# Attention with three full heads, then a maxout layer, on one core: keys and queries of four halves transposed by DMA, a head's long score tile on both row halves of the array, and a new order of all instructions

## The chip, the core and the metric

The kernel runs on 1 core of one Trainium2 chip. The metric is the device time of one execution, in microseconds (us). Before the change it is 176.41 us, the median of 3 runs (176.35 to 176.73).

## The reference

Four batches of 768 tokens have 8 heads of 64 columns. A head is either full (causal attention) or a stream head, which sees the first 4 keys and the last 64. Which heads are full is an input; here there are three of them. The tokens' head outputs are joined to x (3072 x 512), which goes through a maxout layer:

```python
scores = scale * np.matmul(q, k.transpose(0, 1, 3, 2))
mask = np.where(retr[0, :, 0, 0, None, None], full_mask, stream_mask)
a = np.exp(scores - max)                      # masked scores are -1e9
a = a / (np.sum(a, axis=-1, keepdims=True) + 1e-09)
attn = np.matmul(a, v)
...
x = attn.transpose(0, 2, 1, 3).reshape(B * S, H * D)
out = np.maximum(x @ w1, x @ w2) @ w_out      # w1, w2: 512 x 1024; w_out: 1024 x 512
```

All inputs and the output are float32. The kernel works in bfloat16 with float32 sums.

## The kernel before, in words

**Halves.** The work is cut into 8 halves (b, h): batch b, tokens 0 to 383 (h = 0) or 384 to 767 (h = 1). They are taken in the order of `HALVES`: (0,0), (1,0), (0,1), (1,1), (2,0), (2,1), (3,0), (3,1). The heads of a batch go in four pairs, `SLOTS = ("FF", "FS", "SS", "SS")`: pair 0 holds two full heads, pair 1 a full and a stream head, pairs 2 and 3 stream heads. One head of a pair has rows 0 to 63 of the TensorE array, the other rows 64 to 127. n = 4 b + pair numbers the pairs.

**One half.** The loads of q, k and v (`load_half`, L413) fill one of three slots of `ld`. A half in `LONG` takes q and k in one 768 KB transfer each (L426), with runs of 768 bytes; any other half, and every v but the first, takes three 256 KB transfers (L439), with runs of 256 bytes. Casts (`cast_qk`, `cast_v`; L366 on ScalarE, L368 on VectorE and GpSimd) bring them to bfloat16. Then q and k of each pair are transposed, so that the 64 columns of a head lie on partitions. That is done in one of two ways: for the halves in `TURNED_BY_DMA`, (2,1), (3,0) and (3,1), by two DMA transposes per pair, one for q and one for k (`turn_by_dma`, L666); for the other five by TensorE (`turn`, L645, six 128x128 transposes per pair) and a copy out of PSUM (`unturn`). `attend` (L1018) lays the 128x128 score blocks out in tiles of two PSUM banks (`GROUP_A`, `GROUP0`, `GROUP1`). Per tile there are the score matmuls (`scores`, L915), two exponentials (ScalarE, L930), the masks (VectorE, L955), and the sums with v (`weighted`, L980). When a pair is done, VectorE divides by the sums (L997, L1007) and writes x.

**Row halves.** A score matmul has 64 rows. `scores` alternates between the two banks of a tile; where these belong to the two heads of a pair, the two matmuls use different row halves. In `GROUP1`, used for every h = 1, tile 5 holds only blocks of pair 1's full head, so both of its banks use rows 0 to 63.

**The layer.** x is transposed (by TensorE at L1103 for the first three halves, by one DMA transpose at L1122 for the others). The layer is computed as relu(x(w1 - w2)) w_out + x(w2 w_out): `up` (L1206) multiplies by w1 - w2, which VectorE makes at L1139 (`w` in rows), with a relu behind it (L1231, L1233); `down` (L1263) does twelve matmuls of 512 columns per 128 tokens, four on x with w2 w_out (`w2o`) and eight on the relu's output with w_out (`wob`). The product w2 w_out is made once, at the start: VectorE or ScalarE casts w2 (`w2b`), TensorE transposes it (L1156), the transposes are copied out (`w2t`), and 32 matmuls multiply by w_out (L1183).

**What sets the order.** `Order.run` takes a string, `PLAN`: each token names a step, its engine (p TensorE, a ScalarE, v VectorE, g GpSimd, s SyncE) and its PSUM banks. Each engine executes its own steps in this order, and waits only for what they need. A token xN is a dummy matmul of 128 columns (L353) on bank N, which computes nothing that is used; there are 133. SyncE issues nearly all transfers, in the order of its tokens.

Of the kernel before, what the change touches and what calls it, by code (L numbers as in the profile page):

```python
# [22 lines left out]
def f(j, *queries):  # L23
    return tuple(("f", j, i) for i in queries)


def d(i):
    return (("d", i),)
# [10 lines left out]
def one(p, hh, blocks):  # L39
# [47 lines left out]
    ([one(1, 0, f(0, 3, 4, 5) + f(3, 4)), one(1, 0, f(1, 3, 4, 5) + f(3, 5))], []),  # L87
    ([one(1, 0, f(2, 3, 4, 5)), one(1, 1, END1 + d(5))], [(1, 1, 0, 2, 2)]),
# [27 lines left out]
class Order:  # L116
# [38 lines left out]
0s x0*3 1s x0*5 2s x0*36 3s 66a 50v x0*3 28a 64v x0 48g x0 58a x0 68p0 26a 25g x1*2 52p1 56a 69v 44p2 x3 4s  # L155
60p3 53v x4*2 45v x4*5 8s 29a 67g 65v x4*4 57a x4 49g x4*4 27a x4 59v x4*2 70p4 51a x5 46p5 x6 71v x6 54p6 47a
62p7 x0*2 61v x0*2 63a x0 72p01 55v x2*4 74a x2*3 9s 31g x2 30v x2*3 76p24 33g 73a 6s 32v 81p53 85p76 34a 35g
89p10 83a 75v 37g 87a x3*3 84v x3*4 91a x3*2 36g 93p36 90a x0 13s 126v x0*2 40p0 95a 11s 92v 38p1 86a 122v 82a
5g 42p6 41a 39v 123p7 78a 43v 127p5 124a 80v x0 108p0 97p1 128v 77a 99p 139p4 100v 16s 130a 134v 137p6 152p7
101v 94a 135p5 102v 79v 131p2 136a 96v 98p1 103p 88v 138p3 132a 113p 104v 10v 107p5 109p 105v x2*4 7g x2*2  # L160
106v x2*7 110v x2*2 114v x2*2 112v x2*6 111v x2*6 14s 140p 115v 116v 143p 141p 144p 15s 125v 117p2 153p 118a
121v 154p 12g 119p1 142p 120a 145p 215p5 148p 216a 150p 149a 19s 133v 146p 151a 155p 147a 213p0 129v 226p2
214a 156v 224p1 18s 157a 181g 167a 197g 159v 227a 220p5 195v 169a 183v 225a 163p3 173p4 221a 201p6 164v 222p0
202a 174v 187p7 20s 170a 158g 209p2 168a 188v 160g 184a 182g 175p1 223a 165p5 210v 198g 189p3 176a 211p6 196g
17s 166v 190a 203p4 179v 177v 240p70 212a 193v 244p21 204v 247p53 423s 241a 219p6 191v 245a 205v 246a 207v
242a 218p4 249a 243v 229p 248a 251v 21s 250v 252p72 234p 254a 253a 24s 172v 161g 162a 255v 256p10 186a 199g
200v 185a 260p35 264p27 258a 171g 230p 194v 262a 208g 178v 261a 237p 206v 426s 266a 263v 257a 268p0 269p 238a
180v 217p5 259v 265a 239s 192a 270v 267v 273p3 274p 272v 279p7 235a 278p1 275v 427s 292g 271v 280p 309a 284p
228p 276v 293g 319a 285v 281v 308g 277v 299a 296p6 424s 282v 298g 318a 231p 286v 297a 283v 322p2 287v 551s
232a 302p4 323v 290p0 303a 288p3 312p1 289v 291a 359p67 363p52 425s 324v 360a 366p40 326v 340p3 304v 306v 365a  # L170
313v 368a 334p6 22s 437g 453a 452v 336p2 341a 314v 457g 236s 335v 444a 330p0 436a 430v 23s 367a 441v 431v
332p1 361a 445v 337v 338p3 331a 362v 333a 342p6 449a 316v 339v 364a 676s 434g 328p4 443v 451a 450g 369p72 343v
329a 372p01 377p35 428g 435v 550s 371a 380p64 373a 349p2 429v 378a 442v 375v 382a 432p0 379a 438p3 383v 673s
321g 301v 446p4 300a 294g 350p 370a 439v 381a 295g 552s 320g 374a 351p 447v 305g 433a 325g 396p5 307v 397p
327g 310a 448v 384p76 388p31 386a 392p40 440v 398p 671s 311v 393a 399p 376v 354p6 317v 315a 233s 400v 385a
402v 807s 403p4 401v 394a 404p 387v 405p 355p 389a 395v 390a 356p 406v 391v 804s 561a 562g 409p7 407v 411p
571a 408v 410p5 581g 565p0 412v 572a 556v 555g 415p 344p3 357a 554s 413v 416v 566a 414v 345p 418v 352a 417v
559p1 582a 674s 421p4 560a 575p6 346p 576v 422a 806s 419p7 347a 489p05 420v 493p21 490a 496p46 672s 454p3 495a
# [12 lines left out]
620v 748p75 706s 811g 838a 751p64 613p 746a 812v 827v 749a 828v 816s 614p 817v 750a 837v 818v 753a 778p0 752a
615v 754p17 747a 759p54 756a 762p62 841s 716p3 761a 758v 764a 720p7 842s 763a 765v 710p4 755a 721a 712p2 757v
822s 717a 779p 711a 713v 780p 760a 781p 785p6 832s 782v 714p1 783v 784v 786p 715a 787p 766p73 788v 770p42 821s
843v 768a 774p50 845v 789v 726p1 772a 790v 767a 815s 825v 823v 718p3 771a 769v 731p6 775a 831s 833v 835v 776a
773v 724p2 719a 777v 722p7 616s 725a 931s 792p4 723a 797p 791p5 798v 793p 727p 800v 928s 794v 799v 728p 795v
796v 935s 878p03 729v 882p27 885p45 880a 732p 886a 730s 887a 733p 888v 884a 889v 883a 801s 736p1 879a 734v
881v 890p34 894p57 892a 898p20 930s 906p6 895a 893v 907p 911p4 900a 908v 737p 932s 909v 896a 910v 899a 902p50
897v 738p 891a 901v 903a 904a 916p7 905v 739a 912p 917p6 913v 922p 918p 929s 851p2 914v 915v 853p3 923v 852a
919v 925v 933s 855p5 921v 854a 924v 859p0 621s 920v 856v 934s 868p1 860a 847p4 926s 950a 959v 936g 942a 857p2
937g 943a 849p3 958g 951a 858a 861p6 941s 850v 848a 863p7 862a 864p 940s 960a 953v 952g 869p 944a 939v 961a  # L200
957a 938v 965v 870p 945v 949g 865p 947s 871a 978p5 866a 946s 997p02 979v 1001p43 999a 1004p61 970p7 955s 998a
1002a 976p5 1000v 1006a 948v 954s 980p2 971v 1005a 977v 1034p0 1003a 966p4 981a 1035p 963s 967v 1007p17
1010p65 1009a 1036p 1008a 972p3 962s 956v 1012a 1037p 968p2 973v 1011a 735s 1014v 1015p47 1038v 969v 740s
1018p15 1022p36 1016a 1039v 872s 974p2 1040v 1024a 867s 964v 1013v 873p4 1020a 975v 1017a 1021v 1041p0 1023a
1026p65 1019a 1030p27 1025v 1042p 1028a 1043p 874p 1031a 1044v 1046v 1032a 1045v 1047p3 1027a 875p 1033v 1029v
1049p 992p1 876a 1050v 1052v 877s 1048p5 1051v 1053p 993p 1054v 1055v 1056v 994p 1057s 1094v 982p2 995v 983p
996s 1095p7 987p0 1096v 988p 989p 984p 990a 991s 1062p6 985a 1072p4 986s 1063a 1058p3 1073v 1068p5 1059a
1079p1 1069a 1084p0 1060p2 1064p6 1061v 1070p4 1065a 1066p3 1071a 1074p7 1067v 1075p 1080p 1081p 1076p
# [3 lines left out]
1082v 1085p 1083s 1077a 1086p 1078s 1089p5 1087v 1090p 1091p 1088s 1092a 1093a  # L212
# [15 lines left out]
NLD = 3  # L228
NQB = 6
NQK = 8  # L230
# [6 lines left out]
LONG = ((0, 0), (0, 1), (1, 0), (1, 1), (2, 0))  # L237
# [65 lines left out]
def tile_three_full_heads(  # L303
# [109 lines left out]
    def load_half(b, hf, kinds=(0, 1, 2)):  # L413
# [45 lines left out]
        if b in V_BY_DMA:  # L459
            order_ = [(t, i) for t, i in order_ if t < 2]  # L460
# [1269 lines left out]
```

## Time and profile before

| what | value |
|---|---|
| median of 3 runs | 176.41 us (176.35 to 176.73) |
| the profiled execution: span from its first to its last instruction | 175.4 us |
| what the median has beyond that span | 1.0 us |
| instructions | 4945 |
| granted TensorE clock, mean | 0.997 |
| moved by DMA | 36.14 MB, 206 GB/s in the mean |

Times in the trace count from the span's start. A row of the timeline gives a start, a length and the merged instructions; a row of the windows gives, for a stretch, the busy time of each engine with its count of instructions, then the granted clock, the DMA share and GB/s. TensorE's matmuls overlap, and "mean ns of one" is longer than the step from one to the next; the price of a matmul in a row of many is therefore taken from start to start.

### The profile page before, as it was taken

Reading aid. Unit: us, or ns where it says so; the run is one execution under the profiler, and the core shown is the slowest. Engines: PE = TensorE matmul, PEld = TensorE weight load, DVE = VectorE, ACT = ScalarE, POOL = GpSimd, SP = SyncE. Lnnn points to the kernel's source line nnn. Section 1 sums busy time; section 2 is a strip of 40 time slices with the busy share of each in tenths; the row PEclk is TensorE's granted clock in tenths of the full one; section 3 lists DMA queues with packets and bytes.
Section 4 is the critical chain, followed back from the end, with each engine's and each line's share of the span. In section 5 each row is a group of like instructions: output and inputs, shape, how many; then the busy total and the mean of one; then the engine's idle time right before and its main releaser. Section 6 shows DMA issues by size and latency. Waiting matters only on the chain.

```text
span 175.4 us, 4945 instructions
## 1 busy us (share of the span) xinstructions
PE 168.5 (96%) x1795; PEld 105.5 (60%) x1816; DVE 122.0 (70%) x331; ACT 126.3 (72%) x280; POOL 34.2 (19%) x78
## 2 busy tenths in 40 slices
PE   7999799999999999999999999999999999999993
PEld 7976575655665666666656545764565566545542
DVE  5579899686999997887858666666884168941211
ACT  3499807998999998999997669795858598405200
POOL 5732132422414613040200240000012000000000
PEclk9999999999999999999999999999999999999998
DMA  4999999999899999992597993339999334453004
GB/s 129 334 371 389 387 382 333 214 312 298 201 248 258 281 300 211 234 283 71 152 190 192 238 225 76 71 69 237 213 242 176 67 87 153 154 153 122 0 7 179
DMA packets 77661, 36.14 MB, mean 206 GB/s; under 512 B 59202, under 2 KB 72514, under 8 KB 77634
## 3 DMA queue, kind: packets, MB, share of 16 engines
q1 hardware_dynamic: 77488, 35.73, 78.4%
q8 instruction: 15, 0.25, 0.6%
q14 instruction: 12, 0.10, 0.2%
q10 hardware_dynamic: 146, 0.07, 0.1%
HBM read 25.17 MB, written 6.29 MB: 179 GB/s over the span
## 4 chain that ended last, share of the span: by engine, by line
PE 85%; DMA 6%; POOL 3%; issue 2%; DVE 2%; POOLq 0%; ACT 0%; DVEq 0%; SPq 0%; ACTq 0%
PE ps L1263 36%; PE ps L1206 24%; PE ps L915 9%; PE ps L980 8%; DMA ld<-in_moe_w_dram 6%; PE ps L645 3%; PE ps L1183 3%; POOL tab L1605 1%; PE ps L1103 1%; DVE at L955 1%; PE ps L353 1%; DVE x L1007 0%; POOL tab L1619 0%; POOL g L705 0%; POOLq L1670 0%
## 5 line engine op out<-in xcount | busy, mean ns | idle before, releaser
L930 ACT ACTIVATE at<-ps 128x512 bf16<-128x512 f32 (+2 forms) x134 | 64.1, 573 | 6.4 <-PE ps L915 6.2
L1206 PE MATMUL ps<-xt,w 128*128 128x384 bf16 x256 | 45.8, 326 | 0.0
L1263 PE MATMUL ps<-wob,g 128*128 128x512 bf16 (+2 forms) x192 | 44.7, 370 | 0.4
L955 DVE TENSOR_TENSOR at<-at,tab 128x1024 bf16<-128x1024 bf16 (+5 forms) x56 | 29.9, 549 | 10.7 <-ACT at L930 10.3
L1206 PEld LDWEIGHTS <-w 128*128 128x128 bf16 x256 | 23.9, 98 | 16.0 <-issue 0.4
L1263 PEld LDWEIGHTS <-g 128*128 128x128 bf16 x200 | 18.0, 98 | 18.8 <-issue 0.2
L1231 ACT ACTIVATE g<-ps 128x384 bf16<-128x384 f32 x37 | 18.0, 502 | 11.1 <-PE ps L1206 10.0
L1233 DVE TENSOR_SCALAR g<-ps 128x384 bf16<-128x384 f32 x27 | 14.6, 550 | 15.8 <-PE ps L1206 15.7
L1263 PE MATMUL ps<-w2o,xt 128*128 128x512 bf16 (+2 forms) x90 | 23.5, 370 | 0.5
L1007 DVE TENSOR_TENSOR x<-ps,rez 128x192 f32 x64 | 22.7, 355 | 1.6
L368 POOL CAST qb<-ld 128x384 bf16 (+1 forms) x28 | 13.2, 505 | 50.5 <-DMA ld<-in_q_dram 30.6
L366 ACT COPY ot<-ps 128x512 f32<-128x512 f32 (+1 forms) x18 | 10.4, 575 | 17.0 <-PE ps L1263 16.8
L980 PEld LDWEIGHTS <-at 128*128 128x128 bf16 x477 | 18.6, 97 | 6.3 <-DVE at L955 1.2
L980 PE MATMUL ps<-vb,at 128*128 128x65 bf16 x387 | 20.4, 193 | 0.4 <-DVE at L955 0.4
L915 PE MATMUL ps<-qk 64*128 64x128 bf16 (+1 forms) x330 | 18.4, 228 | 0.2
L915 PEld LDWEIGHTS <-qk 64*128 64x128 bf16 x330 | 12.2, 94 | 7.2 <-issue 4.7
L368 DVE COPY qk<-ps 128x384 bf16<-128x384 bf16 (+1 forms) x17 | 11.3, 693 | 3.9 <-PE ps L645 3.8
L1263 PEld LDWEIGHTS <-xt 128*128 128x128 bf16 x100 | 8.9, 97 | 8.5
L366 ACT CAST qb<-ld 128x384 bf16 (+1 forms) x31 | 11.8, 440 | 2.8 <-DMA ld<-in_q_dram 1.7
L353 PE MATMUL ps<-warmer 128*128 128x128 bf16 x133 | 12.1, 256 | 1.4 <-POOL warmer L1655 1.2
L353 PEld LDWEIGHTS <-warmer 128*128 128x128 bf16 x133 | 10.5, 118 | 1.7 <-POOL warmer L1655 1.2
L368 POOL CAST vb<-ld 128x192 bf16 x15 | 5.7, 406 | 24.6 <-DMA ld<-in_v_dram 24.5
(74 smaller groups left out, 161.4 us busy)
## 6 DMA issues: line engine op xcount, KB each, us to landing
ld<-in_v_dram SPq DMA_DIRECT2D x21, 256.0 KB, 5.0
ld<-in_moe_w_dram SPq DMA_DIRECT2D x4, 1024.0 KB, 11.8
out_dram<-ot SPq DMA_DIRECT2D x16, 256.0 KB, 3.4
ld<-in_q_dram SPq DMA_DIRECT2D x5, 768.0 KB, 7.3
ld<-in_k_dram SPq DMA_DIRECT2D x5, 768.0 KB, 8.4
ld<-in_k_dram SPq DMA_DIRECT2D x9, 256.0 KB, 4.5
ld<-in_q_dram SPq DMA_DIRECT2D x9, 256.0 KB, 4.9
ld<-in_moe_w_out_dram SPq DMA_DIRECT2D x4, 512.0 KB, 10.6
```

What stands on the lines that cost most here:

```text
L353: nc.tensor.matmul(banks[e][:, 0:128 * m].rearrange("p (m c) -> p m c", m=m), lhsT=warm, rhs=warm.unsqueeze(1).to_broadcast([128, m, 128]) ...
L366: nc.scalar.copy(out=out, in_=in_)
L368: eng[e].tensor_copy(out=out, in_=in_)
L915: nc.tensor.matmul(to.rearrange("p (i c) -> p i c", c=128), lhsT=lhsT, rhs=q_of(n, i, m)[rows], start=True, stop=True, skip_group_check=True,)
L930: nc.scalar.activation(out=at[:, bk, 0:w], in_=bank(("ps", b, hf, t), part=bk)[:, 0:w], func=ACT.Exp, scale=scale,)
L955: eng[e].tensor_tensor(out=at, in0=at, in1=tbl, op=ALU.mult)
L980: nc.tensor.matmul(po[:, hh, i - NT * hf, :], lhsT=ats[:, T["at", b, hf, t] % NAT, bk, e * 128:(e + 1) * 128], rhs=rhs, start=first, stop= ...
L1007: nc.vector.tensor_tensor(out=xs[:, HALVES.index((b, hf)) % NX, :, bass.ds(heads[2 * p + hh], 1), :], in0=po[:, hh, :, 0:D].unsqueeze(2), ...
L1206: nc.tensor.matmul(bank(key)[:, 0:HALF], lhsT=w[:, kc, fc * 128:(fc + 1) * 128], rhs=xts[:, HALVES.index((b, hf)) % NXT, :, kc, :], start= ...
L1231: nc.scalar.activation(out=g, in_=ph, func=ACT.Relu)
L1233: nc.vector.tensor_scalar_max(out=g, in0=ph, scalar1=0.0)
L1263: nc.tensor.matmul(bank(key)[:, cols], lhsT=lhsT, rhs=(w2o if kind == "x" else wob)[:, c, cols], start=(e == 0), stop=(e == len(steps) - 1),)
```

## The change

1. **Transposes by DMA for a fourth half.** `TURNED_BY_DMA` gets (2,0). For all four halves a single transfer per pair now transposes q and k together: 16 transfers of six blocks instead of 24 of three. For that `qk` is laid out in the order q of h = 0, k of h = 0, k of h = 1, q of h = 1.
2. **(2,0) leaves `LONG`**: its q and k come in three 256 KB transfers each instead of one of 768 KB.
3. **Tile 5 of `GROUP1` on both row halves.** A new SyncE transfer, `second_rows`, copies k of h = 0 and q of h = 1 of pair 1's full head from partitions 0 to 63 to partitions 64 to 127 of a new tile `cp`. The second bank of tile 5 takes its operands from there (blocks "c"), and so uses rows 64 to 127. One block changes places with tile 6.
4. **Smaller things.** Dummies: 133 of 128 columns become 27 of 512 (token y). The cast of w2 may go to GpSimd. `vb` rows are 66 columns instead of 68, `tab` is smaller. For h = 1, q and k swap places in a slot of `ld`.
5. **`PLAN` and `LAST` are made anew**: another order, another engine for many steps.

```diff
-    ([one(1, 0, f(0, 3, 4, 5) + f(3, 4)), one(1, 0, f(1, 3, 4, 5) + f(3, 5))], []),
-    ([one(1, 0, f(2, 3, 4, 5)), one(1, 1, END1 + d(5))], [(1, 1, 0, 2, 2)]),
+    ([one(1, 0, f(0, 3, 4, 5) + f(3, 4)), one(1, 0, c(1, 3, 4, 5) + c(2, 3))], []),
+    ([one(1, 0, f(2, 4, 5) + f(3, 5)), one(1, 1, END1 + d(5))], [(1, 1, 0, 2, 2)]),
...
-                    self.dummy(int(spot))
+                    self.dummy(int(spot), 4 if token[0] == "y" else 1)
...
 PLAN = """
-0s x0*3 1s x0*5 2s x0*36 3s 66a 50v x0*3 28a 64v x0 48g x0 58a x0 68p0 26a 25g x1*2 52p1 56a 69v 44p2 x3 4s
+0s y0 1s y0 2s y0 y1*3 y2*3 3s y3*3 y4 56a 66v y4 26a 48v y4 64a 28v y5*2 25g y5 y6 50g y6 58g 52p0 44p1 4s 60p2
...
-LONG = ((0, 0), (0, 1), (1, 0), (1, 1), (2, 0))
+LONG = ((0, 0), (0, 1), (1, 0), (1, 1))
...
-TURNED_BY_DMA = ((2, 1), (3, 0), (3, 1))
+TURNED_BY_DMA = ((2, 0), (2, 1), (3, 0), (3, 1))
...
-    VW = D + 4
+    VW = D + 2
...
-    qks = keep.tile([128, NQK, 2, S], BF16, name="qk")
+    qks = keep.tile([128, NQK, 4, HALF], BF16, name="qk")
+    cps = keep.tile([128, NCP, 2, HALF], BF16, name="cp")
...
+    def place(t, hf):
+        return t if t == 2 else t ^ hf
...
-    def turn_by_dma(n, hf, t):
+    def turn_by_dma(n, hf):
         def emit(_):
             nc.sync.dma_start_transpose(
-                out=qks[:, n % NQK, t, HALF * hf:HALF * hf + HALF].rearrange("f (i c) -> f i c", c=128),
-                in_=qbs[:, T["qb", n, hf] % NQB, t].rearrange("p n h d -> p (n h d)"),
+                out=qks[:, n % NQK, 2 * hf:2 * hf + 2].rearrange("f t (i c) -> f (t i) c", c=128),
+                in_=qbs[:, T["qb", n, hf] % NQB].rearrange("p t n h d -> p (t n h d)"),
             )
...
+                    if blk[0] == "c":
+                        rows = slice(64, 128)
+                        lhsT = cps[rows, b % NCP, 0, 128 * blk[1]:128 * blk[1] + 128]
...
+    def second_rows(b):
+        n = b * HP + [p for p, kind in enumerate(SLOTS) if kind == "FS"][0]
+        def emit(_):
+            nc.sync.dma_start(
+                out=cps[64:128, b % NCP], in_=qks[0:64, n % NQK, 1:4:2],
+            )
...
-                {"DVE": 0.61, "ACT": act(1024)},
+                {"DVE": 0.61, "ACT": act(1024), "POOL": 1.3},
...
-    tab = consts.tile([128, 16 * 128], BF16, name="tab")
+    tab = consts.tile([128, 11 * 128], BF16, name="tab")
```

What the new order does at three places follows; rows that would only repeat are left out. First, TensorE at the start, where w2 w_out is made (L1183 before, L1134 after) and the first `up` begins (L1206, L1157). Before, from the end of a run of 29 dummies:

```order
L353 MATMUL ps_157<-warmer 128x128
L1183 LDWEIGHTS w2t
L1183 MATMUL ps_161<-wob,w2t 128x512
...
L1206 LDWEIGHTS w_139
L1206 MATMUL ps_160<-xt,w_139 128x384
...
L1183 MATMUL ps_158<-wob,w2t 128x512
```

After:

```order
L1134 MATMUL ps_163<-wob,w2t 128x512
L1134 LDWEIGHTS w2t
L1134 MATMUL ps_161<-wob,w2t 128x512
...
L1157 LDWEIGHTS w_139
L1157 MATMUL ps_156<-xt,w_139 128x384
```

The dummies are gone from this place, and the last eight matmuls of w2 w_out, which stood behind the first four of `up`, now stand ahead of it.

Second, TensorE in tile 5 of (0,1), `ps` being the tile's two banks. Before:

```order
L915 LDWEIGHTS qk
L915 MATMUL ps_158<-qk 128x384
L915 MATMUL ps_160<-qk 128x384
L915 MATMUL ps_158<-qk 128x128
L915 MATMUL ps_160<-qk 128x128
```

After:

```order
L845 LDWEIGHTS qk
L845 MATMUL ps_156<-qk 128x384
L845 LDWEIGHTS cp
L845 MATMUL ps_163<-cp 128x384
L845 MATMUL ps_156<-qk 128x128
L845 MATMUL ps_163<-cp 128x128
```

The four matmuls are the same in number and size; those of the second bank read `cp`.

Third, SyncE around the first DMA transposes of q and k (L668 before, of (2,1); L617 after, of (2,0) and the first of (2,1)). Before:

```order
L1291 DMA out_dram<-ot 128x512
L668 DMA_TRANSPOSE qk<-qb 128x3x128 x3
L439 DMA ld<-in_v_dram 128x8x64
L1291 DMA out_dram<-ot 128x512
L668 DMA_TRANSPOSE qk<-qb 128x3x128
L439 DMA ld<-in_q_dram 128x8x64
L1122 DMA_TRANSPOSE xt<-x 128x12x128
```

After:

```order
L447 DMA ld<-in_q_dram 128x8x64
L617 DMA_TRANSPOSE qk<-qb 128x6x128
L1242 DMA out_dram<-ot 128x512
L617 DMA_TRANSPOSE qk<-qb 128x6x128
L447 DMA ld<-in_k_dram 128x8x64
L617 DMA_TRANSPOSE qk<-qb 128x6x128
L1073 DMA_TRANSPOSE xt<-x 128x12x128
```

Five transposes of six blocks now stand ahead of the transpose of x of (1,1), with three loads and two stores between them, where four of three blocks stood.

More of the change, by code (lines that the diff above doesn't have):

```diff
@@ new lines, in prepare @@
+        old_qb = last_turn.get(hist_qb[-NQB], ()) if len(hist_qb) >= NQB else ()
+        T["qb", n, hf] = len(hist_qb)
+        hist_qb.append((n, hf))
+        cs = []
+        for hh in range(2):
+            for lo, hi in ((0, 1), (1, 2)) if (b, hf) in SPLIT and (b, hf) not in SIX else ((0, 2),):
+                cs.append(cast := op(
+                    dict(CAST_QK) if hi - lo == 2 else dict(CAST_V), cast_qk(n, hf, hh, lo, hi),
+                    [*(o for t in range(lo, hi) for o in loads[b, hf, t]), registers, *old_qb],
+                    tag=f"cast{b}.{hf}.{p}", rank=rank_of("cast", b, hf, p), port=("DVE", "POOL"),
+                    bias=BIAS if b else None,
+                ))
+                leaves((b, hf), range(lo, hi), [cast])
@@ new lines, in prepare @@
+        casts[n, hf] = cs
+        old_v = last_w.get(n - NQK, ())
+        vs = []
+        if (b, hf) in SPREAD:
+            if p == 0:
+                T["spread", b, hf] = spread_half(b, hf)
+            vs = T["spread", b, hf]
+        for hh in range(2) if (b, hf) not in SPREAD else ():
+            vs.append(op(
+                dict(CAST_V), cast_v(n, hf, hh), [*loads[b, hf, 2], registers, *old_v],
+                tag=f"vcast{b}.{hf}.{p}", rank=rank_of("vcast", b, hf, p), port=("POOL", "DVE"), bias=BIAS if b else None,
+            ))
@@ new lines, in prepare @@
+        leaves((b, hf), (2,), vs if (b, hf) not in SPREAD else ())
+        key = ("pt", n, hf)
+        old_s = last_s.get(n - NQK, ())
+        if (b, hf) in TURNED_BY_DMA:
+            last_turn[n, hf] = turned[n, hf] = [
+                op(
+                    {"SP": TURN_ISSUE}, turn_by_dma(n, hf), [*cs, *old_s], data=DMA_TURN * 2 * NT,
+                    tag=f"turn{b}.{hf}.{p}", rank=RANK["turn"],
+                )
+            ]
+        else:
+            last_turn[n, hf], turned[n, hf] = [], []
+            tq = None
+            for lo, hi in ((0, 1), (1, 2)) if (b, hf) in SPLIT else ((0, 2),):
+                if tq is not None and (b, hf) in SIX:
@@ L857, in prepare @@
+                last_turn[n, hf].append(tq)
+                un = op(
+                    {"DVE": 0.08 + (0.41 if (b, hf) in LONG else 0.2) * m, "ACT": 0.065 + 0.325 * m},
+                    unturn(n, hf, lo, hi), [tq, *old_s],
+                    frees=[key],
+                    tag=f"unturn{b}.{hf}.{p}", rank=rank_of("unturn", b, hf, p),
+                    bias=None,
+                )
+                turned[n, hf].append(un)
         ks, vmix = [], list(vs)
@@ L1030, in attend @@
                         deps += mixed_k[n, 0] + (mixed_k[n, 1] if hf else [])
[L1031 removed]
+            copied = any(blk[0] == "c" for bk in group[t][0] for *_, blk in bk)
+            if copied:
+                deps.append(second_rows(b))
+            serial = not copied and all(hh == 0 for bk in group[t][0] for _, hh, _ in bk)
             cost = mm(*[128] * len(group[t][0][0])) * (2 if serial else 1)
@@ L1325, in tile_three_full_heads @@
             weights = prep_weights()
-        if b not in CAST_BY_DMA:
-            load_half(b, hf, [t for t in range(3) if (b, hf, t) not in loads])
+        load_half(b, hf, [t for t in range(3) if (b, hf, t) not in loads])
         order.shift = STEP * at
```

308 lines of the change are left out of this document (98 added, 210 removed).

## The prediction

> **What bounds the kernel now.** I read the page first: busy shares, the slices and the chain of waits.
>
> ```profile
> PE 168.5 (96%) x1795; PEld 105.5 (60%) x1816; DVE 122.0 (70%) x331; ACT 126.3 (72%) x280; POOL 34.2 (19%) x78
> PE   7999799999999999999999999999999999999993
> DMA  4999999999899999992597993339999334453004
> PE 85%; DMA 6%; POOL 3%; issue 2%; DVE 2%; POOLq 0%; ACT 0%; DVEq 0%; SPq 0%; ACTq 0%
> ```
>
> TensorE is busy 96% of the span and is 85% of the chain. The DMA engines are full up to slice 18 of 40, about 79 us, and not after. A busy TensorE may be doing dummies, so I then asked for windows that part the start from the rest, and one of the rest up to where the DMA engines stop being full.
>
> ```profile
> 10.00:27.87 17.87, 16.57 (x229) 11.80 (x230) 16.05 (x32) 12.71 (x22) 5.55 (x8) 1.00 1.05 381
> 27.87:172.39 144.52, 143.19 (x1469) 85.38 (x1485) 99.97 (x271) 108.95 (x246) 22.57 (x50) 1.00 0.77 183
> 27.87:79.10 51.23, 50.68 (x567) 32.13 (x571) 43.98 (x109) 46.79 (x106) 15.85 (x35) 1.00 1.05 262
> ```
>
> The timeline of TensorE tells what these bounds are: 27.87 is the first `up`, 172.39 the end of the last matmul.
>
> ```profile
> 1.16 5.51 PE L353 MATMUL ps<-warmer 128*128 128x128 bf16 x50 [1.16 <-POOL warmer L1655]
> 22.13 1.78 PE L353 MATMUL ps<-warmer 128*128 128x128 bf16 x29
> 27.87 0.81 PE L1206 MATMUL ps<-xt,w 128*128 128x384 bf16 x4
> 171.78 0.61 PE L1263 MATMUL ps<-wob,g 128*128 128x128 bf16 x8
> ```
>
> From the first `up` to the end TensorE stands idle for 1.33 of 144.52 us. There, work taken off TensorE comes off the time, if nothing else becomes late. Before it, TensorE does dummies (29 of them at 22.13), so the start is set by something else. The rows of VectorE and ScalarE ahead of the first `up` say by what.
>
> ```profile
> 21.62 1.43 DVE L368 CAST wob<-ld 128x1024 bf16<-128x1024 f32 x1
> 23.83 1.53 DVE L1007 TENSOR_TENSOR x<-ps,rez 128x192 f32 x4
> 25.29 5.46 DVE L1139 TENSOR_TENSOR w<-ld 128x1024 bf16<-128x1024 f32 x4
> 26.12 1.67 ACT L366 COPY xt<-ps 128x1024 bf16<-128x1024 bf16 x2 [4.04 <-PE ps L1103]
> ```
>
> VectorE works through masks, casts and divisions until 25.36 (23.83 + 1.53), and starts w1 - w2 directly behind them, four pieces of 1.36. ScalarE copies the transposed x until 27.79; then `up` starts.
>
> The profiled execution has a span of 175.4; the median of the runs, 176.41, is 1.0 above it, and I take the same 1.0 for after. The trace of one execution cannot tell less than about 0.2% (0.35 us) from no change, nor can the runs.
>
> **Part by part. Off TensorE behind the first `up`.** The prices are from the chain of waits, whose pieces do not overlap (start, length, count), and from two rows of the timeline.
>
> ```profile
> 28.69 1.73 PE ps L1183 x8
> 50.69 5.31 PE ps L1206 x32
> 58.28 1.00 PE ps L645 x18
> 69.92 0.86 PE ps L1263 x4
> 79.75 0.22 PE L915 MATMUL ps<-qk,kx 64*128 64x128 bf16 x2
> 79.81 0.22 PE L915 MATMUL ps<-qk 64*128 64x128 bf16 x2
> ```
>
> - The transposes of (2,0): 18 take 1.00, so 0.056 each; 24 go: **-1.34**. Their four copies out of PSUM go from VectorE and ScalarE too; those lie beside TensorE, and I count nothing.
> - Tile 5 of `GROUP1`: a matmul of 384 columns takes 5.31 / 32 = 0.166. Two matmuls of 128 columns on different row halves take 0.06 together (79.75 to 79.81), as long as one transpose alone: the pair runs side by side. Per batch, one matmul of 384 and one of 128 columns vanish behind their partners, 0.22; four batches: **-0.89**.
> - The last eight matmuls of w2 w_out, which stand behind the first four matmuls of `up` now (28.69), move ahead of it: **-1.73**, if the first `up` stays where it is.
>
> **The first `up`.** From the landing of k on (8.28 in ScalarE's row below), VectorE's list up to the last division loses the cast of w_out (1.43 above) and three casts of w2; it gains four casts of q or k, one of v's rows, one copy of q or k, two of w2t and one of v, which I price as w2t's.
>
> ```profile
> 8.28 1.11 ACT L366 CAST qb<-ld 128x192 bf16 x4 [1.03 <-DMA ld<-in_k_dram]
> L368 DVE CAST w2b<-ld 128x1024 bf16<-128x1024 f32 x3 | 2.1, 692 | 1.1 <-DMA ld<-in_moe_w_dram 1.1
> L368 DVE COPY qk<-ps 128x384 bf16<-128x384 bf16 x11 | 5.7, 552 | 2.1 <-PE ps L645 2.1
> L368 DVE COPY w2t<-ps 128x1024 bf16<-128x1024 bf16 x1 | 0.7, 680 | 0.0
> L368 DVE CAST qb<-ld 128x192 bf16 x7 | 2.1, 341 | 0.8 <-DMA ld<-in_q_dram 0.8
> POOL wob L368 <- DMA ld<-in_moe_w_out_dram: 11.2, 3, 4.4
> ```
>
> Lost: 1.43 + 2.1 = 3.5. Gained: 5 x 0.34 + 0.55 + 3 x 0.68 = 4.3; since the means of one count overlaps, I take 0.5 net, and the last division at 25.9. Behind it now come the fourth copy of w2t (0.68) and the smaller half of x's (0.35, half of w2t's), then the first piece of w1 - w2 (1.36): 28.3. VectorE has 17.87 - 16.05 = 1.8 idle us in that window; if the new order needed none of them, it is 26.5. On the other side are three casts of w_out that move to ScalarE, on whose exponentials VectorE waits, and 20 long dummies ahead of the first transposes (at 0.11 per 128 columns, as in the first row of dummies, they last until 10 us, where k lands at 8.28). I allow 1.0 for these. So 26.5 to 29.3; I take 28.2: **+0.3**. The eight groups of `up` then follow the pieces of w1 - w2, 1.36 per two groups, where TensorE needs 8 x 0.166 = 1.33: **+0.2** over all.
>
> **Transfers.** The copy to `cp` is not in the trace. Between the last transpose of pair 1 and tile 5 the order leaves TensorE over 5 us in each batch. The nearest rows for its duration are a store and a load.
>
> ```profile
> out_dram<-ot SPq DMA_DIRECT2D x14, 128.0 KB, 1.8
> ld<-in_q_dram SPq DMA_DIRECT2D x9, 256.0 KB, 4.9
> qk<-qb SPq DMA_TRANSPOSE x24, 2.4
> xt<-x SPq DMA_TRANSPOSE x5, 4.2
> 25.00:30.00 5.00, 1.00 1.08 343
> 70.00:75.00 5.00, 1.00 1.05 240
> ```
>
> 1.8 to 4.9 is covered; nearer to the store's, since it moves 98 KB. A transpose of six blocks lies between those of three and twelve, 2.4 and 4.2: about 3.0. A 256 KB load costs 1.09 at the 240 GB/s of a stretch that has only these, a 768 KB load 2.29 at 343. Ahead of the first transpose of q and k, SyncE issued 29 transfers of 256 KB (23 loads, six stores) and eight of 768 KB, 29 x 1.09 + 8 x 2.29 = 49.9, which is nearly the 51.23 of the full window. After, it is 27 and six and two copies: 43.7, so the first transpose can go about 6 us earlier, near 73. TensorE comes to the first scores of (2,0) earlier as well:
>
> ```profile
> 86.71 0.44 PE ps L915 x12
> 84.72 0.27 PE ps L980 x8
> 93.20 1.30 PE ps L1206 x8
> 151.92 0.36 PE ps L980 x12
> 153.37 1.41 SPq L1122 DMA_TRANSPOSE xt<-x  x1
> xt<-x SPq DMA_TRANSPOSE x1, 3.2
> ```
>
> 86.71 + 0.3 + 0.2 - 1.73 - 1.34 - 0.44 (two tiles 5), less 3.7 of work that the order puts behind them (three groups of `down`, 29 sums with v at 0.03, a score tile): 80.0. The first transpose lands by 76; the fourth, with stores and loads between, by 81 or 82, and is wanted some 5 us after the first. Then x of (1,1): from its last sums (84.99) to its first `up` (93.20) TensorE now has 8.2 us of other work, after only 5.2 (four groups of `down` at 0.86, six score tiles, 14 sums). In (3,1) the sums ended at 152.28, the transpose was issued at 153.37 and landed after 3.2; with the 4.2 of the median that is 5.3. So a wait of 0 to 2 here, and 0 to 2 on (2,0). I take **+1.0** for both and all other new waits; the ends are 0 and 4.
>
> Sum: -1.34 - 0.89 - 1.73 + 0.3 + 0.2 + 1.0 = -2.5, so 176.4 - 2.5 = **173.9**. With the first `up` at 26.5 and no waits it is 171.2; with it at 29.3 and waits of 2, 176.0. The forecast's own range is 172.3 to 175.6, short of the corners, where both ends would have to meet.
>
> **The rivals.**
>
> *The DMA queue takes the gain (18%).* The wait that takes the place of the removed work is that for the transposes of (2,0) and of x of (1,1). For it: the queue is full to 79 us whatever TensorE does, and TensorE comes nearly 7 us earlier. Against: 6 us of transfers leave the queue's head. With waits of 2.2 to 4.0 instead of 1.0 it gives 175.1 to 176.9.
>
> *ScalarE stands at w_out, slower (12%).* GpSimd waited 11.2 us for w_out in three casts, with nothing behind it that was urgent. Now ScalarE does three of the four, and what stands behind them waits too. ScalarE has 17.87 - 12.71 = 5.2 idle us in that window, of which the moved steps take about 2. If it stands at w_out for all 11.2, the first `up` comes 11.2 - 3.2 = 8 late instead of 0.3: 181.6. It decides from a first `up` 2.8 late, past 30.7, where the gain is gone. Against: five exponentials stand behind the first cast, none behind the others.
>
> *The clock falls at the start, slower (5%).* The first 50 dummies took 0.11 each, the 29 later ones 0.06: TensorE works at half rate until it has been busy for some us. The dummies between 10 and 24 us are gone; if TensorE falls back to half rate there, the 16.57 busy us of the window, some 13 of them real work, take 26 and the first `up` comes near 38, 183.7. Granted clock is 1.00 in the window, so the page shows no loss with dummies, and nothing without. The Trainium skill ("TensorE: Matmul & The Clock Gate", Part 1) says that the half rate is the default, released by a busy window of about 3.4 us and restored by an idle one. By that rule it takes a gap of that length; I see gaps of about 1 us in the order.
>
> *The start gains more (5%):* 171.2 to 172.3, by the lower end above. *The copy does not bring the banks side by side (3%):* 0.89 stays, 174.8.
>
> **How the numbers follow.** The forecast has 57%. 172.3 to 176.9 holds it, the queue's rival and the 174.8, and leaves out 5% below and about 15% above. Faster by over 0.2%, under 176.06: 57 + 5 + 3 and 9 of the queue's 18, 74%. Within 0.2%, to 176.76: 8 of the queue's, 8%. Slower: 12 + 5 and 1, 18%.
>
> **What would show it.** Right: the first `up` between 26.5 and 29.3, all of w2 w_out ahead of it; no L594 transposes of (2,0); the row of `cp` starting with that of `qk`; TensorE idle for about 2 us behind the first `up`. Wrong: dummy-like step times of 0.11 after 13 us; a wait on `qk` or `xt` of over 2 us between 75 and 95; ScalarE waiting for w_out past 20 us.

## The result, and the profile after

The kernel after takes 177.12 us (median of 14 runs, 176.68 to 178.82); the kernel before, beside it on the same chips, 176.66 us (14 runs, 175.86 to 177.00). The ratio is 1.0056, with a 95% interval of 1.0031 to 1.0081: slower by about 1.0 us, where 2.5 us faster was forecast. (The medians alone differ by 0.5; the ratio goes by all runs.) The runs of after lie in two groups, nine from 176.7 to 177.5 and five from 178.1 to 178.8.

The span of the profiled execution is 175.3 us, 0.1 less than that of before. That comparison misleads: every run of after is 1.7 us longer than its span, while the forecast added 1.0 to a span. A second profile of before (experiment e1) has a span of 174.7, and its run was also some 1.8 us longer. The execution that the prediction was read from was therefore a long one, by about 0.7 us. In these records the spans agree with the times: after is the longer one.

The page of after, the lines that answer to those shown of before:

```profile
PE 166.6 (95%) x1686; PEld 95.3 (54%) x1686; DVE 116.4 (66%) x334; ACT 120.4 (69%) x267; POOL 34.7 (20%) x84
PE   7899899999799999999989999999999999999992
DMA  4999999999989998998999899898997450135505
PE 54%; DMA 21%; DVE 13%; ACT 4%; issue 3%; SPq 1%; DVEq 1%; ACTq 0%
```

TensorE is still busy 95%, but it is only 54% of the chain that ended last, where it was 85%. DMA has gone from 6% to 21% and VectorE from 2% to 13%. These shares differ from one execution to the next (second profiles, e1: TensorE 61% in after, 82% in before), but the direction is the same. The DMA engines are at 80% or more up to slice 30, about 131 us, and no longer only to 79.

The timeline of TensorE at the start, and tile 5 of (0,1):

```profile
26.25 1.89 PE L1134 MATMUL ps<-wob,w2t 128*128 128x512 bf16 x8
27.98 5.36 PE L1157 MATMUL ps<-xt,w 128*128 128x384 bf16 x32
55.90 0.33 PE L845 MATMUL ps<-qk 64*128 64x384 bf16 x1
55.91 0.33 PE L845 MATMUL ps<-cp 64*128 64x384 bf16 x1
```

All of w2 w_out stands ahead of the first `up`, which starts at 27.98 (27.87 before, 28.2 forecast). The two banks of tile 5 start 0.01 us apart. No transposes of (2,0) are left on TensorE. So the change does what it says.

Then the windows from the first `up` to the last matmul: after, and below it the second profile of before (length, busy PE with its matmuls, busy PEld, DVE, ACT and POOL, granted clock, DMA share, GB/s).

```profile
27.98:172.18 144.20, 141.29 (x1455) 82.14 (x1453) 94.89 (x268) 102.58 (x233) 25.76 (x61) 1.00 0.85 192
```

```profile
27.79:171.74 143.95, 143.89 (x1487) 85.37 (x1485) 98.13 (x271) 108.78 (x246) 22.55 (x50) 1.00 0.76 184
```

The stretch should have lost 2.8 us (3.96 removed, 0.2 and 1.0 added); it grew by 0.25. TensorE stands idle for 2.91 us in it, before for 0.06. The 1.33 us that the prediction read as idle were matmuls missing from the record: it has 1469 there, this one 1487. Counted from start to start, what a step takes beyond the usual step of its kind sums to about 4.0 us in after and 0.5 in e1's before; with another choice of what is usual it is 4.6 and 0.8. So nearly all of the 3.96 us came back as waits. The largest waits of after that the timeline names:

```profile
47.86 0.62 PE L1054 MATMUL ps<-tab,x 128*128 128x128 bf16 x8 [0.93 <-DVE x L937]
69.01 0.84 PE L1054 MATMUL ps<-tab,x 128*128 128x128 bf16 x12 [0.36 <-DVE x L937]
90.63 0.66 PE L1157 MATMUL ps<-xt,w 128*128 128x384 bf16 x3 [0.48 <-DMA xt<-x]
112.00 0.81 PE L1157 MATMUL ps<-xt,w 128*128 128x384 bf16 x4 [0.27 <-DVE g L1184]
121.06 0.38 PE L845 MATMUL ps<-qk 64*128 64x128 bf16 x7 [0.31 <-DVE x L937]
159.02 1.30 PE L1157 MATMUL ps<-xt,w 128*128 128x384 bf16 x7 [0.23 <-DMA xt<-x]
```

The first of them is not at a transfer. It is for VectorE's last division of (1,0), at 47.8 us, and 1.9 of the 2.6 us in these rows are VectorE's.

### The profile page after: what moved, and what is told of

Same layout as the page of the kernel before. It is cut to its first block, busy times and chain, and to the rows that moved or that the text cites. A ratio compares the mean times of both kernels' runs of the same rounds, so it can differ in the third digit from the quotient of the medians.

```text
span 175.3 us, 4688 instructions
## 1 busy us (share of the span) xinstructions
PE 166.6 (95%) x1686; PEld 95.3 (54%) x1686; DVE 116.4 (66%) x334; ACT 120.4 (69%) x267; POOL 34.7 (20%) x84
## 4 chain that ended last, share of the span: by engine, by line
PE 54%; DMA 21%; DVE 13%; ACT 4%; issue 3%; SPq 1%; DVEq 1%; ACTq 0%
PE ps L1157 22%; PE ps L1214 19%; DVE x L937 8%; DMA xt<-x 6%; DMA qk<-qb 5%; DMA ld<-in_moe_w_dram 5%; PE ps L910 4%; PE ps L845 4%; DMA ld<-in_k_dram 4%; ACT at L860 2%; PE ps L594 2%; DVE rez L927 2%; PE ps L1054 1%; DVE at L885 1%; PE ps L1134 1%
## 5 line engine op out<-in xcount | busy, mean ns | idle before, releaser
L860 ACT ACTIVATE at<-ps 128x512 bf16<-128x512 f32 (+2 forms) x134 | 65.3, 570 | 13.6 <-PE ps L845 9.1
L1214 PE MATMUL ps<-wob,g 128*128 128x512 bf16 (+2 forms) x200 | 46.8, 371 | 0.1
L1157 PE MATMUL ps<-xt,w 128*128 128x384 bf16 x256 | 45.1, 326 | 1.1 <-DMA xt<-x 0.9
L885 DVE TENSOR_TENSOR at<-at,tab 128x1024 bf16<-128x1024 bf16 (+5 forms) x56 | 28.0, 532 | 12.9 <-ACT at L860 12.6
L1157 PEld LDWEIGHTS <-w 128*128 128x128 bf16 x256 | 24.1, 98 | 17.8 <-DMA xt<-x 1.0
L369 POOL CAST qb<-ld 128x384 bf16 (+1 forms) x32 | 15.2, 502 | 49.1 <-DMA ld<-in_q_dram 28.1
L367 ACT COPY ot<-ps 128x512 f32<-128x512 f32 (+1 forms) x14 | 8.2, 602 | 11.3 <-PE ps L1214 10.8
L369 POOL CAST vb<-ld 128x192 bf16 x22 | 7.9, 381 | 26.4 <-DMA ld<-in_v_dram 26.3
L369 DVE COPY ot<-ps 128x512 f32<-128x512 f32 (+1 forms) x11 | 7.1, 647 | 6.9 <-PE ps L1214 6.6
L367 ACT CAST qb<-ld 128x192 bf16 (+1 forms) x22 | 8.4, 417 | 3.5 <-DMA ld<-in_q_dram 1.8
L369 DVE CAST qb<-ld 128x192 bf16 (+1 forms) x26 | 8.5, 363 | 2.4 <-DMA ld<-in_k_dram 1.5
L927 DVE RECIPROCAL rez<-ps 128x6 f32<-128x6 f32 x32 | 5.4, 181 | 6.5 <-PE ps L910 5.2
```

Source lines behind the costliest of these rows:

```text
L367: nc.scalar.copy(out=out, in_=in_)
L369: eng[e].tensor_copy(out=out, in_=in_)
L860: nc.scalar.activation(out=at[:, bk, 0:w], in_=bank(("ps", b, hf, t), part=bk)[:, 0:w], func=ACT.Exp, scale=scale,)
L885: eng[e].tensor_tensor(out=at, in0=at, in1=tbl, op=ALU.mult)
L927: nc.vector.reciprocal(out=z, in_=po[:, :, :, D])
L1157: nc.tensor.matmul(bank(key)[:, 0:HALF], lhsT=w[:, kc, fc * 128:(fc + 1) * 128], rhs=xts[:, HALVES.index((b, hf)) % NXT, :, kc, :], start= ...
```

## Experiments: two references

**e1.** Both kernels unchanged.

> The kernel before, unchanged, beside itself: what a ratio of two equal kernels looks like, and its spans. The prediction took 1.0 us for the time outside the span (176.41 less 175.4); every run of the kernel after shows 1.7. If the changed kernel really spends 0.7 more outside its span, the runs here show spans of about 175.4 with 1.0 outside; if the profiled execution of before was merely a long one, they show 1.7 outside and spans of about 174.9. Ratio 0.998 to 1.002 either way.

> The kernel after, unchanged, a second time: ratio to before 1.003 to 1.008. Its 14 runs fell into two groups, 176.7 to 177.5 and 178.1 to 178.8. If a wait for a transfer makes the groups, they come again, about one run in three in the upper one, and a trace of the upper group shows one wait of TensorE that is about 1.5 us longer.

Before: ratio 0.9998 (0.9980 to 1.0016), span 174.7. After: 1.0052 (1.0034 to 1.0070), six runs from 177.3 to 177.7 and one at 178.0. The time outside the span is the same in both kernels. What makes the two groups stayed open here.

## Experiments: what the removed work is worth

Theory S says that TensorE still sets the time and that the parts saved less than was counted; theory W, that what is taken off TensorE comes back as waits, because the work of other engines ends hardly earlier. Within W, theory D puts it on the added transfers and theory V on VectorE's masks and divisions.

**e14** leaves the last eight matmuls of w2 w_out out of before, and **e15** the transposes of (2,0) with their four copies out of PSUM: the two largest terms of the sum, alone, in the order of before.

```diff
             def emit(_, kc=kc, key=key, c=c):
+                if c == 3:
+                    return
...
```

```diff
         def emit(_):
+            if 8 <= n < 12 and hf == 0:
+                return
             pt = bank(("pt", n, hf, lo), BF16)
...
```

> The kernel before without the last eight matmuls of w2 w_out, the ones that stand behind the first four of the layer's first product and that the change moves ahead of it (so w2 w_out lacks a quarter of its sum): 1.73 us less for TensorE right behind 28.69 us, the term as the prediction priced it. As priced: 1.5 to 1.7 us faster than before. If the divisions of (1,0), whose x was taken over within 0.1 us of its end, set that stretch: 0.1 to 0.6 us faster, with TensorE waiting up to 1.6 us at 47 us.

> The kernel before without the 24 transposes of (2,0) on TensorE and their four copies out of PSUM (its scores are then of older q, k): what the change takes off TensorE there, without the transfers that it puts in their place. As priced: 1.3 us faster than before. If what is taken off early comes back as waits for the transfers and VectorE: 0.3 to 0.8 us.

e14: ratio 0.9950 (0.9930 to 0.9969), 0.88 us (0.5 to 1.2) of the 1.73. e15: 0.9972 (0.9957 to 0.9987), 0.49 us (0.2 to 0.8) of the 1.34. Neither reached its price. In e14 x of (1,0) was divided 1.2 us earlier than in before (47.11 for 48.27), without a wait at 47 us; by steps, TensorE waited 0.5 us for w1 - w2 at 29 us instead.

**e2** undoes tile 5 of `GROUP1` in after.

```diff
-                    if blk[0] == "c":
-                        rows = slice(64, 128)
-                        lhsT = cps[rows, b % NCP, 0, 128 * blk[1]:128 * blk[1] + 128]
-                    elif blk[0] == "x":
+                    if blk[0] == "x":
...
-            nc.sync.dma_start(
-                out=cps[64:128, b % NCP], in_=qks[0:64, n % NQK, 1:4:2],
-            )
+            return
```

> After, with the second bank of tile 5 again from rows 0 to 63 and without the copy: four times 0.22 us of TensorE's time come back. Theory W (what was taken off TensorE came back as waits, because the divisions and the transfers behind it end hardly earlier than before): 0.0 to 0.4 us slower than after, and TensorE's waits in the trace shorter by 0.4 or more. Theory S (TensorE still sets the time, the parts of the change just saved less than was counted): 0.8 to 0.9 us slower than after, waits as in after. If the copy itself costs something, as a transfer that other transfers wait for, it is faster than after.

Ratio 1.0091 (1.0060 to 1.0121) beside 1.0052 (1.0034 to 1.0070) of after: 0.7 us slower by the ratios, 0.5 by the medians, of 0.88. The copy is worth having; whether at its full price these runs do not tell.

**e3 and e4** leave 6.9 us of `down` out, spread over all halves, in after and in before; **e9 and e10** leave 1.73 us of the same work out of before at two places.

```diff
                     kind, c = steps[e]
+                    if kind == "x" and ti == 0:
+                        continue
...
```

> After, without the product of x and w2 w_out for the first 128 tokens of each half: 32 matmuls of 512 columns, 6.9 us of TensorE's work, nothing else changes. Theory S: 6.5 to 6.9 us faster than after. Theory W: at most half of it, 1.5 to 3.5 us faster than after, with about 4 us more of waits in TensorE.

> The kernel before, without the product of x and w2 w_out for the first 128 tokens of each half: the same 6.9 us of TensorE's work as were left out of after in e3, where 3.1 us of them came off the time. If before has its second limit farther behind TensorE than after has (theory D below, its DMA engines are not full behind 79 us): 4 to 6 us faster than before. If both have it at the same distance, that is, if divisions and exponentials set it, which are the same in both (theory V): 2.5 to 3.5 us faster than before.

> The kernel before, without x times w2 w_out for the first 128 tokens of (0,0) and (1,0): 8 matmuls, 1.73 us of TensorE's work between 37 and 62 us. As the prediction argued (work taken off TensorE comes off the time): 1.5 to 1.7 us faster than before. If the divisions of (1,0) and (0,1) are only just in time in before too: 0.2 to 0.9 us faster, with TensorE waiting for x at 48 or 68 us.

> The same 1.73 us left out of before at (2,0) and (2,1), between 110 and 145 us. As the prediction argued: 1.5 to 1.7 us faster than before. If the transposes of x and the exponentials behind it are only just in time: 0.2 to 0.9 us faster.

e3: 0.9881 (0.9855 to 0.9908), 3.0 us less than after's 1.0052, so 44% of the work; slightly more than half stayed as waits. e4: 0.9783 (0.9768 to 0.9798), 3.8 us, 56%: between what the two theories expected, so before has its second limit only a little farther off than after. e9: 0.9976 (0.9964 to 0.9989), 0.4 us or 24%. e10: 0.9938 (0.9919 to 0.9957), 1.1 us or 63%. In e9 TensorE now waits for q or k and for x of (1,0) at 47 us, and by steps 0.5 us more for x of (0,1) at 68, as after does for x:

```profile
46.95 0.84 PE L645 MATMUL ps<-tab,qb 128*128 128x128 bf16 x12 [0.27 <-ACT qb L366]
48.21 0.84 PE L1103 MATMUL ps<-tab,x 128*128 128x128 bf16 x12 [0.42 <-DVE x L1007]
```

Theory S, that TensorE alone sets the time, has fallen, already for before.

## Experiments: what TensorE waits for now

These runs part theories D and V. **e5** shortens the stores, **e6** leaves the masks out, **e7** loads (2,0) in long pieces, **e12** leaves out the DMA transposes of (2,0) and **e13** those of all four halves, all in after.

```diff
+                m = n // 4 if HALVES.index((b, hf)) < 6 else n
...
-                        out=out[r0:r0 + 128, lo:lo + n], in_=ots[:, number % NOUT, lo:lo + n]
+                        out=out[r0:r0 + 128, lo:lo + m], in_=ots[:, number % NOUT, lo:lo + m]
```

```diff
         def emit(e):
+            return
             at = ats[:, T["at", b, hf, t] % NAT, first:first + count, cols]
```

```diff
             def emit(_):
+                if (b, hf) == (2, 0) and t < 2:
+                    if i == 1:
+                        nc.sync.dma_start(
+                            out=lds[:, s, at],
+                            in_=src[b, :, rows, :].rearrange("h (p n) d -> p h (n d)", p=128),
+                        )
+                    return
```

```diff
     def turn_by_dma(n, hf):
         def emit(_):
+            if n < 12 and hf == 0:
+                return
```

> After, with only the first quarter of each store's columns written for the first six halves: as many transfers in the same order, some 13 us less work for each DMA engine, as much as the change has added. Theory D (the added transfers keep the DMA engines full to 130 us, and the transposes of q, k and x land late, which TensorE waits for): 1.5 to 3 us faster than after, and no wait for x or q, k left over 0.2 us behind 85 us. Theory V (VectorE's masks and divisions are late): at most 0.5 us faster.

> After, without the masks, 28 us of VectorE's work; nothing else changes. Theory V: 1.5 to 3 us faster than after, and the waits for x at 47 and 68 us gone. Theory D: those two waits go as well, but what they give is waited for behind 85 us, so at most 1 us faster than after.

> After, with q and k of (2,0) loaded in one transfer of 768 KB each again, as in before, in place of six of 256 KB; this leaves the tokens of (2,0) in another order, so that the scores of this half are of other tokens. Packets of 768 bytes take 42 ns and those of 256 bytes 21, so 62 us of packets less over 16 engines: 3.9 us less for each DMA engine. Theory D: 0.7 to 1.5 us faster than after. Theory V: within 0.3 of after.

> After, with the four transfers that transpose q and k of (2,0) left out (its scores are then of older q, k); casts, loads and all else stay. Theory D (the transposes on the DMA engines, and what they hold up, cost what TensorE saved by them): 1.0 to 2.0 us faster than after, the gain behind 85 us. If they are hidden: within 0.3 us of after.

> After, with all 16 transfers that transpose q and k left out, so that scores of the last four halves are of older q, k. It bounds what these transfers can cost: TensorE's waits behind 85 us were 2.0 to 2.3 us, 1.0 to 1.9 of them for transposed q, k or x, so 1.5 to 3 us faster than after if theory D holds, at most 1.0 if these waits only stand for others (banks that divisions and relus free late) that come in their place.

| run | ratio to before | against after (1.0052) |
|---|---|---|
| e5, short stores | 1.0009 (0.9987 to 1.0031) | -0.8 us |
| e6, no masks | 1.0044 (1.0022 to 1.0066) | -0.1 us, within the interval |
| e7, long loads | 1.0041 (1.0022 to 1.0061) | -0.2 us, within the interval |
| e12, no transposes of (2,0) | 1.0032 (1.0013 to 1.0052) | -0.4 us, the intervals overlap |
| e13, none at all | 1.0140 (1.0098 to 1.0182) | +1.6 us |

In e5 the waits for transfers sum to 0.6 us by steps, from 1.4 in e1's after; the two for x of (1,0) and (0,1) stay:

```profile
48.07 0.62 PE L1054 MATMUL ps<-tab,x 128*128 128x128 bf16 x8 [1.15 <-DVE x L937]
69.23 0.84 PE L1054 MATMUL ps<-tab,x 128*128 128x128 bf16 x12 [0.38 <-DVE x L937]
```

So the added transfers cost at least 0.8 us, half of what theory D asked for. It may be more: e5 took away less than the change had added. The packets' time is 150.0 us for each DMA engine in e1's after, 142.7 in e5 and 136.4 in e1's before, and from 79 to 130 us the engines are as full in e5 as in after (DMA share 1.00, before 0.74). e7 took 2.5 us for each engine, not the expected 3.9. What the transposes of (2,0) alone cost is not clear of the noise. The masks cost nothing measurable: without them x of (1,0) came 0.7 us earlier (47.40 for 48.13), and the end did not move. Of theory V the divisions are left; no run makes them shorter. e13 does not answer its question. Its VectorE stood still in a copy of k, which takes 0.18 us as a rule, while GpSimd did six casts in a row, and TensorE waited 2.24 us for the divisions behind it; e13's rows stand in the last section. It shows one thing: the waits at 111 and 112 us, 1.3 us by steps in e1's after, are gone in it.

**e11** turns q and k of a pair by two transfers again.

```diff
-            nc.sync.dma_start_transpose(
-                out=qks[:, n % NQK, 2 * hf:2 * hf + 2].rearrange("f t (i c) -> f (t i) c", c=128),
...
+            for t in range(2):
+                nc.sync.dma_start_transpose(
+                    out=qks[:, n % NQK, 2 * hf + t].rearrange("f (i c) -> f i c", c=128),
```

> After, with q and k of a pair transposed by two transfers of three blocks again, 32 in place of 16. Six blocks landed 3.8 us (median) after the issue, three blocks in before 2.4. If the longer single transfer makes q and k late: 0.3 to 0.8 us faster than after. If SyncE's time matters (1.2 us more for each pair, 19 us in all): 0.5 to 2 us slower. If neither, within 0.3 us of after: then one transfer for both is worth nothing here.

193.5 us (190.8 to 194.9), 1.0905 (1.0856 to 1.0954): 15 us slower than after, far past the expected 2. SyncE's own rows of e11, of its longest run, point to the reason:

```profile
83.49 2.48 SPq L618 DMA_TRANSPOSE qk<-qb  x2
86.01 0.58 SPq L447 DMA_DIRECT2D ld<-in_q_dram  x1
86.64 2.86 SPq L618 DMA_TRANSPOSE qk<-qb  x2
89.56 0.56 SPq L447 DMA_DIRECT2D ld<-in_k_dram  x1
90.26 2.48 SPq L618 DMA_TRANSPOSE qk<-qb  x2
```

Each issue keeps SyncE for 1.24 us, with three blocks as with six (median 1.29 in the profile of after), and SyncE issues without a pause. The transfers' order is then set by SyncE's time, although the DMA engines are only 60% full from 80 to 90 us (91 to 94% from 100 to 120). One transfer for both is the part of the change without which a fourth half could not be turned this way in this order. The prediction counted it at nothing.

## Experiments: filling the waits

**e8** moves steps at three places of TensorE's waits; **e16** moves six of GpSimd's casts of (3,1) to VectorE, because in e2, e7, e8 and e13 a VectorE instruction had stood still in that row of casts; **e17** joins e16 and two places of e8. Of the edits to `PLAN`, one place of e8 and the one of e16:

```diff
-302p3 297a 323v 311g 288p2 300g 303a 312p4 301g 289v 290p0 366p71
+302p3 297a 323v 311g 312p4 366p75 288p2 300g 303a 301g 289v 290p0
```

```diff
-727a 932g 876v 929s 886a 936g 893p04 930s 888v 889p25 895a 880p37 951g
+727a 876v 929s 886a 893p04 930s 888v 936v 951v 932v 931v 944v 950v 889p25
```

> After, with TensorE's order (and the steps that go with it) changed at three places of its waits, no work added or removed. At 47 us the last transposes of q, k and one score tile of (0,1) go ahead of the transposes of x of (1,0), whose last division comes late; at 110 us two groups that need no transposed q, k go ahead of the score tiles that wait for them, and VectorE's relu ahead of its copy of k that waits for the same transfer; at 120 us a group of the layer goes ahead of a score tile that waits for its bank. The waits there are 1.3, 1.0 to 1.25 and 0.5 of the 3.9 us. Theory W (the lost time is these waits, of work in the wrong place): 0.8 to 1.8 us faster than after, so level with before or faster. If what is filled there is waited for behind it, because the transfers behind it set the end: at most 0.3 us faster than after.

> After, with six of the eight casts of q and k of (3,1) moved from GpSimd, where seven of them stand in a row from 123.9 to 128 us, to VectorE, which is idle from 124.7 to 127.3; nothing else changes. In three variants of after (e2, e7, e8) one VectorE mask or copy that began in this row of casts took 3.0 to 3.1 us in place of 0.2 to 0.55, and so did a copy in e13; in the two traces of after it began ahead of the row and took its usual time. Theory G (VectorE's instruction stands still until GpSimd's row of casts ends, and whether it does so makes the two groups of after's times, 1.5 us apart): no run in an upper group, the spread of the runs under 1.0 us, and 0.3 to 1.0 us faster than after in the median. If the row is harmless in after: within 0.3 us of after, with the same spread.

> The same, and two of the three places of e8 (47 and 110 us; the group at 120 us stays where after has it). e8's trace had the 3.1 us mask, so its 178.7 did not tell what filling the waits is worth. If waits in the wrong place are the loss: another 0.5 to 1.2 us faster than e16, level with before or faster. If what is filled is waited for behind it, for the transposed x at 90 us above all: within 0.4 us of e16.

e8: 1.0118 (1.0086 to 1.0151), 1.2 us slower than after, not faster. Its trace has a mask that stood still, and a new wait of TensorE behind it:

```profile
124.32 3.55 DVE L888 TENSOR_TENSOR at<-at,tab 128x768 bf16<-128x768 bf16 x2 [2.51 <-ACT at L863]
127.48 0.54 PE L913 MATMUL ps<-vb,at 128*128 128x65 bf16 x12 [1.03 <-DVE at L888]
```

e16: 1.0054 (1.0036 to 1.0072), as after; four of its twelve runs lie at 177.9 to 178.2. So theory G has fallen as the cause of the two groups, and the row of casts costs after nothing. e17: 1.0062 (1.0045 to 1.0079), the same as e16. At 47 us it waits less, and nothing came of it:

```profile
47.71 0.39 PE L848 MATMUL ps<-qk 64*128 64x384 bf16 x4
48.40 0.84 PE L1057 MATMUL ps<-tab,x 128*128 128x128 bf16 x12 [0.29 <-DVE x L940]
```

x of (0,1) is divided at 69.4 us in e17, at 69.2 in e16 without the fill. The waits show where TensorE runs ahead of the others; filling these two did not end the program earlier. None of the three beat before.

## Why the prediction was wrong, by its own steps

**"There, work taken off TensorE comes off the time, if nothing else becomes late."** This step failed, and it failed in before itself. The three terms, priced at 1.73, 1.34 and 0.89, are worth 0.88 (e14), 0.49 (e15) and 0.5 to 0.7 (e2): about 2.0 of 3.96 if they add up, which no run tested. The matmuls did go. What did not move as much is what stands beside them. The trace of before had a sign of it, in rows that the prediction did not use, VectorE's divisions of (1,0) and the transposes of x behind them:

```profile
46.81 1.89 DVE L1007 TENSOR_TENSOR x<-ps,rez 128x192 f32 x5
48.75 0.45 PE L1103 MATMUL ps<-tab,x 128*128 128x128 bf16 x5
```

The divisions end at 48.70, and TensorE takes x at 48.75. A TensorE that comes earlier waits there, unless the divisions move as far. In e14 they came 1.2 us earlier, and TensorE lost its time at 29 to 32 us instead, by steps 0.5 for w1 - w2 and 0.3 for q or k. After:

```profile
45.87 1.93 DVE L937 TENSOR_TENSOR x<-ps,rez 128x192 f32 x5
```

They end at 47.80, 0.9 earlier than in the row before and 0.5 earlier than in e1's before (48.27), while 1.73 was priced. One reason may lie in the order (no run tests it): the first score tile of (1,0) starts at 37.21 in after, behind all 32 matmuls of `up`, and at 36.24 before.

```profile
37.21 0.29 PE L845 MATMUL ps<-qk 64*128 64x128 bf16 x4
```

```profile
36.24 0.62 PE L915 MATMUL ps<-qk 64*128 64x128 bf16 x15
```

**The new waits, "+1.0 for both and all other new waits; the ends are 0 and 4".** By steps they measure 4.0 against 0.5, so 3.5 (3.8 by the other count): inside the ends, but 1.0 was the wrong value. The forecast expected them at transfers alone. Of the two places that were named, x of (1,1) holds 0.55 in after and 0.07 in e1's after, (2,0) hardly any. The sum's corners took 2 for the waits at most, although the end for them was 4; with 4 the slow corner is 178.1, past what was measured. (As added, both corners are 0.1 too low: 171.3 and 176.1.)

**Transfers.** The forecast took 3.0 us for a transpose of six blocks, and an issue of the first at 73. The issue was right (72.4), the duration not; the third row is the window from 79 to 130 us in after, the fence behind it the same of e1's before:

```profile
qk<-qb SPq DMA_TRANSPOSE x16, 4.0
xt<-x SPq DMA_TRANSPOSE x5, 3.8
79.00:130.00 51.00, 49.89 (x525) 28.17 (x524) 33.83 (x103) 37.49 (x88) 10.87 (x25) 1.00 1.01 208
```

```profile
79.00:130.00 51.00, 51.00 (x578) 29.92 (x575) 36.99 (x112) 40.86 (x97) 4.19 (x11) 1.00 0.74 163
```

The sum had taken away transfers ahead of the first transpose, and added none for the stretch behind it. There the loads of (2,0) in short pieces and its transposes add 9216 packets of 256 bytes and take away 2048 of 768; the copies to `cp` add 512 of 768 (the share of the 16 engines is 85.4% in e1's after, 78.1% in its before, 13.5 us each). The DMA engines are full from 79 to 130 us, where they were at 74%. e5 prices a bit more than half of that at 0.8 us. SyncE's issuing is not what differs here: its rows sum to 44.7 of these 51 us in e1's after and 44.2 in its before.

**What held.** The first `up` (+0.1, forecast +0.3), the copy, the transposes gone, the granted clock of 1.00. The rival "the DMA queue takes the gain", at 18%, named the right kind of event and too small a place; 176.9 was the range's upper end.

**What stays open.** After is 0.9 us slower than before, although its removed work is worth 2.0. Of these 2.9 us, at least 0.8 are the transfers'. What remains, up to 2, lies in the rest of the transfers' load and in the new order, and no run parts these or shows which move of the order costs how much. By the traces of e1 the second half of the program is where after falls behind: its first `up` of (1,1) is 2.0 us earlier (90.35 for 92.39), its last division of (2,0) 2.3 us later (102.42 for 100.13), that of (3,1) 2.8 later (155.47 for 152.65). By steps, 1.4 us of after's waits, and 2.0 of those of e1's after, lie between 102 and 122 us. In the new order most sums with v of (2,0) stand behind seven of the eight groups of that `up`, before they stood partly ahead; putting them back was not tried. The two groups of after's times stay unexplained as well.

## What to carry to other kernels

An engine that is busy 96% of the span need not set the time alone: in this tuned order several engines arrived together, and the row to read is the handover, how long a result has lain there when the engine takes it. If that is 0.05 us, work taken off the engine ahead of it is worth only as much as the other side moves with it (here half of 1.73 us in e14, a quarter in e9); leaving a piece of work out, at the very place, prices this in one run. Compare the count of matmuls in the trace with that of another trace before you read 1% of idle time as idle.

## What the runs showed of the hardware

**Waits of 2 to 3 us can be followed by half of TensorE's rate.** In e13 TensorE waited 2.24 us, did one matmul of 128 columns, and waited 0.57 us more. Four matmuls of 512 columns take 0.86 us from start to start elsewhere. The last row is the window of 120 to 126 us.

```profile
122.05 0.21 PE L846 MATMUL ps<-qk 64*128 64x128 bf16 x1 [2.24 <-DVE x L938]
122.83 0.38 PE L846 MATMUL ps<-qk 64*128 64x128 bf16 x7 [0.57 <-DVE x L938]
124.41 1.91 PE L1215 MATMUL ps<-w2o,xt 128*128 128x512 bf16 x4
120.00:126.00 6.00, 3.38 (x16) 1.39 (x16) 3.79 (x8) 2.77 (x8) 2.14 (x5) 0.80 0.37 73
```

The group in the third row takes 1.71 us to the start of the next (126.12), and the granted clock is 0.80 in the window. In e11 eight matmuls of `up` took 2.74 us (1.47 in after) behind a wait of 2.04, with one of 0.33 shortly ahead of it. Waits of 0.9 to 1.2 at 47 us did nothing of the kind. The Trainium skill ("TensorE: Matmul & The Clock Gate", Part 1) says that the half rate comes back after an idle window of about 3.4 us; here less idle time than that was enough.

**GpSimd's casts can hold up VectorE.** VectorE's copy of 128 columns in e13, and beside it GpSimd's own copy, which began first, and its casts:

```profile
118.87 2.87 DVE L369 COPY kx<-qk 128x128 bf16<-128x128 bf16 x1
```

```profile
118.70 0.73 POOL L369 COPY vx<-vb 64x660 bf16<-64x660 bf16 x1 [1.50 <-ACT vb L367]
119.38 2.75 POOL L369 CAST qb<-ld 128x384 bf16 x6
```

The copy, 2.7 us longer than usual, ends at 121.74, as the last of the six casts begins (0.45 us apart). The Trainium skill ("SBUF — State Buffer", Who interferes with whom) says that the two engines share a pair of ports as an exclusive lock, and that the one that comes second stands still for the other's instruction. The trace agrees, but VectorE's copy stood through six instructions (GpSimd's copy and five casts), not one. In e16, with these casts on VectorE, no such row is left.
